# A gated linear attention with a feed-forward block on one core: eight small products over 128 rows instead of 32, and a new order table

## The chip, the cores and the metric

The kernel runs on one core of a Trainium2 chip. The metric is the time on the device in microseconds (us). Five engines work side by side, each through its own list in order: PE (matrix products, with the loads of its weights shown apart as PEld), DVE (vector work), ACT (activation functions, through tables that must be loaded), POOL (general work) and SP (here only the issuing of DMA transfers). PE writes to eight accumulation banks, called `banks`.

## What is computed

```python
mag = np.sqrt(a_re * a_re + a_im * a_im)
scale = np.minimum(mag, 0.999) / (mag + 1e-06)
...
for t in range(S):
    new_re = ar * S_re - ai * S_im
    new_im = ar * S_im + ai * S_re
    kv = np.einsum('bhd,bhe->bhde', k[:, :, t], v[:, :, t])
    S_re, S_im = (new_re + kv, new_im)
    y[:, :, t] = np.einsum('bhd,bhde->bhe', q[:, :, t], S_re)
...
xn = (x - mu) / np.sqrt(var + 1e-06) * g_ln
ch = np.maximum(xn @ w_ch1, 0.0) @ w_ch2
return (x + ch)
```

There are 4 batches of 8 heads, 768 steps and a head dimension of 48; x joins the heads to rows of 384, and the two weight matrices are 384 x 1536 and 1536 x 384. All inputs and the output are float32.

## The kernel before

**Tiling.** The 768 steps of a batch are cut into six chunks of 128. Two chunks (R = 2) make a pair P, three pairs make a batch, so there are 12 pairs and 24 chunks n. The recurrence is turned into products: with running sums of the logarithm of the decay and of the phase, a chunk's attention is a masked product of scaled queries and scaled keys, and a state G carries what earlier chunks left. Pair 0 is worked on in two halves of four heads (names such as `e.0.1`), all others whole (`e.3.0`).

**The steps of a pair,** by their names in the code and the lines where they are written:

- loads on SP: `are`, `aim` (L438), `k`, `q`, `vf` (L397)
- decays and phases: `ln`, `iv` (ACT, L441, L443), `r`, `r2`, `u`, `l`, `lc`, then on PE `dec` (L470), a running sum made by a product with the constant triangle u_e, whose exponentials are `e` and `en` (ACT, L474); `th` (ACT), `ph` (PE, L485 with pick and L489 with u_th), `car` (the phase carried to the next pair), `sin`, `cos`, with `qt` (PE, L514) or `abs` in between
- `ke`, `qe`, `ks`, `qs` multiply keys and queries by these; they run on DVE or POOL
- `dps` (PE, L565): eight small products, one per head, that turn the last row of `e` into a column; `decc` copies it to `dec`, which scales the state
- `kT`, `qT` (PE transposes, L584) and their copies `ksT`, `qsT`; `am` (L607), masked by `atm` on DVE; `gm` (L631) and the state `G`; `y` (L668, L671) and its copy `x`
- the feed-forward block: `bn`, `rstd`, `xtr` (PE, L689) with its copy `xT`, `mm1` in three groups of 512 columns (L722), `relu` into h (ACT L734 or DVE L736), `mm2` (L746), `ot` and, where POOL adds, `oa`, and the store `st` (L767).

A copy with the engine letter S in the table is a DMA transpose on SP's queue instead of a PE transpose and a copy (L589, L695); then the PE transpose isn't in the table.

**Once in the program.** Constants are made on POOL: u_e (`ue`), `pick`, `mask`, `ident`, zeros (`pad`, `zdec`), `car0`; `uth` on DVE is u_e over two pi. `wl.0` and `wl.1` are the two weight loads from POOL (L352, L354). `wp` (PE, L377) and `wc` (DVE, L381) fold the norm into the first weight matrix, which must be done before `mm1` can use it. `warm` are fillers: products on u_e of 512 columns (`warm.w`, L780) and of 256 (`warm`, L776) that nothing reads.

**The order.** PLAN is a table written out. Each entry is `step:engine bank`, and each engine runs its entries in the order of the table; waits between engines follow from the data. `@name` adds a wait: this step begins only when the step `name` is over. In the table before, the opening of PE's list reads

```
warm.w25:P2 warm.w26:P2 warm.w27:P2 warm.w28:P2 warm.3:P2@car.0.0 ... dec.0.0:P2
... wl.0:G@ke.0.0.0 ... mm1.0.1.0:P0 ... wl.1:G@mm1.0.1.0
```

Tiles come in rings (two or three buffers of most kinds), so a load of a later pair can be issued only when the step that read the buffer last is over.

Of the kernel before, what the change touches and what calls it, by code (L numbers as in the profile page):

```python
# [43 lines left out]
warm.w8:P0 warm.w9:P0 warm.w10:P0 warm.w11:P0 warm.w12:P0 warm.w13:P0 warm.w14:P0 warm.w15:P0 warm.w16:P0 warm.w17:P0
warm.w18:P0 warm.w19:P0 warm.w20:P0 warm.w21:P0 warm.w22:P0 warm.w23:P0 warm.w24:P0 warm.0:P0 warm.1:P0 warm.2:P0
ph.0.0:P1 aim.2.0:S r2.1.0:G@r2.0.0 ph.0.1:P0 q.0.1:S car.0.1:V0 car.0.0:V1 tab.log.2:A u.0.0:A u.0.1:A l.0.0:V
q.0.0:S u.1.0:A lc.0.0:V l.0.1:V warm.w25:P2 warm.w26:P2 warm.w27:P2 warm.w28:P2 warm.3:P2@car.0.0 warm.w29:P2
warm.w30:P2 warm.w31:P2 warm.4:P2 warm.5:P2 warm.6:P2 dec.0.0:P2 vf.0.1:S lc.0.1:V en.0.0:A2 l.1.0:V k.0.0:S ln.2.0:A
lc.1.0:V iv.2.0:A q.1.1:S warm.w32:P3 warm.w33:P3 warm.w34:P3 warm.w35:P3 warm.w36:P3 warm.w37:P3 warm.7:P3 warm.8:P3
dec.1.0:P4 pad.ks.1:G@lc.1.0 e.0.0:A2 r.2.0:V ph.1.0:P6 q.1.0:S en.1.0:A4 e.1.0:A4 dec.0.1:P2 r2.2.0:V k.1.1:S  # L50
qe.0.0.0:V e.0.1:A2 car.1.0:V6 are.3.0:S en.0.1:A2 warm.w38:P3 warm.w39:P3 warm.9:P3 warm.10:P3 warm.11:P3 dps.0:P4
v.0:V u.2.0:A qe.0.1.0:V aim.3.0:S decc.0:V4 ke.0.1.0:V q.2.0:S ke.0.0.0:V wl.0:G@ke.0.0.0 l.2.0:V tab.trig.3:A
sin.0.1:A0 q.2.1:S sin.0.0:A1 warm.w40:P3 warm.w41:P3 warm.w42:P3 warm.w43:P3 warm.12:P3@u.2.0 warm.w44:P3 warm.w45:P3
warm.w46:P3 warm.w47:P3 warm.w48:P3 warm.13:P3@ke.0.0.0 warm.14:P3 warm.15:P3 qt.0.1:P0 sin.1.0:A6 dps.1:P4 lc.2.0:V
qt.0.0:P1 ks.0.0.1:V dec.2.0:P2 qs.0.1.1:V cos.0.0:A1 qe.1.0.0:V cos.0.1:A0 qt.1.0:P6 qs.0.0.1:V th.2.0:A qs.0.0.0:V
qs.0.1.0:V ks.0.1.1:V cos.1.0:A6 warm.w49:P0 warm.16:P0 warm.17:P0 qT.1:P0 ks.0.0.0:V ks.0.1.0:V qT.0:P1 qsT.1:V0
decc.1:A4 ke.1.0.0:G@ks.0.1.0 kT.1:P5 qsT.0:V1 kT.0:P6 gm.0:P0 qe.1.0.1:V tab.log.4:A e.2.0:A2 qs.1.0.0:V ksT.1:V5
G.0:A0 ke.1.0.1:G@qs.1.0.0 en.2.0:A2 ksT.0:V6 warm.w50:P1 warm.w51:P1 warm.w52:P1 warm.w53:P1 warm.w54:P1 warm.18:P1
warm.19:P1 warm.20:P1 gm.1:P0 am.1:P4 ks.1.0.0:V ln.3.0:A ph.2.0:P2 ks.1.0.1:V iv.3.0:A atm.1:V4 qs.1.0.1:G@ks.1.0.1
kT.3:P6 kT.2:P7 G.1:V0 y.1:P4 ksT.2:V7 am.0:P0 wgc:G tab.trig.5:A sin.2.0:A2 qT.2:P5 k.2.0:S atm.0:V0 x.1:A4  # L60
warm.21:P7 qt.2.0:P2 xtr.1:P4 qsT.2:V5 cos.2.0:A2 wp.1:P7 vf.1.1:S r.3.0:G xT.1:V4 y.0:P0 ksT.3:A6 wc.1.2:V7 am.2:P2
vf.1.0:S qT.3:P1 wc.1.1:V7 x.0:A0 wp.0:P4 pad.qs.2:G k.2.1:S wc.1.0:V7 th.3.0:A xtr.0:P0 wp.2:P5 r2.3.0:G atm.2:V2
qsT.3:A1 are.4.0:S ph.3.0:P6 xT.0:A0 wc.2.1:V5 aim.4.0:S am.3:P2 qe.2.0.1:G car.3.0:A6 mm1.0.1.0:P0 wc.2.0:V5
sin.3.0:A6 are.5.0:S mm1.0.1.1:P0 atm.3:V2 wl.1:G@mm1.0.1.0 v.1:A qt.3.0:P6 vf.2.0:S relu.0.1:A0 ke.2.0.0:G wc.2.2:V5
gm.2:P2 y.2:P3 G.2:V2 cos.3.0:A6 ke.2.0.1:G mm1.0.2.0:P0 wc.0.2:V4 x.2:A3 y.3:P5 qe.2.0.0:G wc.0.0:V4 gm.3:P2 x.3:A5
mm1.0.2.1:P0 wc.0.1:V4 ks.2.0.1:G xtr.2:P3 xtr.3:P5 xT.2:A3 mm1.0.0.0:P6 xT.3:V5 relu.0.2:A0 bn.1:V mm1.1.0.1:P4
ks.2.0.0:V mm1.0.0.1:P6 bn.0:V qs.2.0.0:G@ks.2.0.0 mm1.1.2.0:P0 relu.0.0:V6 tab.log.6:A u.3.0:A kT.4:P3 mm1.1.0.0:P4
one:G ksT.4:V3 ln.4.0:A mm1.1.2.1:P0 qs.2.0.1:V relu.1.0:A4 gs.3:V2 mm1.1.1.1:P6 l.3.0:V iv.4.0:A kT.5:P2 qT.5:P5
relu.1.2:A0 lc.3.0:V mm1.1.1.0:P6 aim.5.0:S ksT.5:V2 G.3:G@lc.3.0 qT.4:P3 qsT.5:V5 relu.1.1:A6 dec.3.0:P0 qsT.4:V3
vf.2.1:S am.5:P4 e.3.0:A0 r.4.0:V am.4:P6 en.3.0:A0 dps.3:P3 atm.5:V4 mm2.1.0:P2 are.6.0:S r2.4.0:A mm2.1.1:P2  # L70
atm.4:V6 vf.3.0:S u.4.0:A mm2.1.2:P2 mm2.0.0:P0 rstd.0:A l.4.0:V ln.5.0:A k.3.0:S mm2.0.1:P0 lc.4.0:V iv.5.0:A
mm2.0.2:P0 decc.3:V3 k.3.1:S ot.1:V2 dec.4.0:P6 v.2:A r.5.0:G@lc.4.0 bn.3:V mm2.3.0:P5 e.4.0:A6 ot.0:V0 q.3.1:S
gm.4:P1 bn.2:V y.4:P3 en.4.0:A6 mm2.3.1:P5 q.3.0:S r2.5.0:G G.4:V1 ln.6.0:A mm2.3.2:P5 x.4:V3 vf.3.1:S iv.6.0:A y.5:P0
bn.4:V xtr.4:P1 mm2.2.0:P4 ke.3.0.0:G k.4.1:S x.5:V0 u.5.0:A xT.4:V1 mm2.2.1:P4 ke.3.0.1:G st.0:S xtr.5:P0 mm2.2.2:P4
xT.5:V0 rstd.1:G l.5.0:V k.4.0:S mm1.2.1.1:P0 tab.trig.7:A th.5.0:A mm1.2.1.0:P0 qe.3.0.1:V aim.6.0:S th.4.0:A
qe.3.0.0:V mm1.2.2.1:P2 relu.2.1:A0 qs.3.0.1:V q.4.0:S mm1.2.2.0:P2 ks.3.0.0:V q.4.1:S ph.4.0:P6 qs.3.0.0:V
relu.2.2:A2 ks.3.0.1:V are.7.0:S qT.6:P0 lc.5.0:V car.4.0:A6 bn.5:V kT.6:P1 ke.4.0.1:G@lc.5.0 abs.4.0:A6 ph.5.0:P2
ot.2:V4 q.5.1:S oa.3:A5 ke.4.0.0:G@lc.5.0 ksT.6:V1 sin.4.0:A6 kT.7:P4 qsT.6:V0 r.6.0:G vf.4.0:S qT.7:P1 cos.4.0:A
ksT.7:V4 mm1.2.0.0:P6 vf.4.1:S abs.5.0:A2 qsT.7:V1 mm1.2.0.1:P6 v.3:G sin.5.0:A2 dec.5.0:P0 relu.2.0:V6 st.2:S
cos.5.0:A qe.4.0.1:G am.7:P4 am.6:P2 th.6.0:A atm.7:V4 are.8.0:S ks.4.0.0:G gm.6:P6 mm2.4.0:P7 G.6:A6 mm2.4.1:P7  # L80
r2.6.0:A st.1:S atm.6:V2 mm2.4.2:P7 ot.3:G aim.7.0:S dps.4:P4 gm.7:P6 qe.4.0.0:G st.3:S decc.4:V4 y.7:P3 G.7:V6 y.6:P2
tab.log.8:A u.6.0:A mm2.5.0:P5 x.7:V3 rstd.2:G ks.4.0.1:V mm2.5.1:P5 x.6:A2 q.5.0:S en.5.0:A0 l.6.0:V xtr.6:P6 k.5.1:S
xtr.7:P2 kT.9:P4 v.4:A xT.6:V6 mm2.5.2:P5 xT.7:V2 lc.6.0:V e.5.0:A0 vf.5.1:S qs.4.0.1:V mm1.3.1.0:P2 ln.7.0:A ot.4:V7
qs.4.0.0:G@qs.4.0.1 dec.6.0:P0 ot.5:V5 mm1.3.1.1:P2 iv.7.0:A bn.7:V mm1.3.0.0:P6 ksT.9:A4 relu.3.1:V2 r.7.0:G qsT.8:S
qT.9:P5 en.6.0:A0 mm1.3.0.1:P6 qsT.9:V5 k.5.0:S e.6.0:A0 kT.8:P2 relu.3.0:V6 qe.5.0.1:G am.9:P4 st.4:S ln.8.0:A
mm1.3.2.1:P0 qe.5.0.0:G q.6.0:S atm.9:V4 r2.7.0:A mm1.3.2.0:P0 qs.5.0.0:G iv.8.0:A gm.8:P3 ph.6.0:P6 aim.8.0:S G.8:V3
u.7.0:A ksT.8:V2 y.9:P4 q.6.1:S relu.3.2:V0 qs.5.0.1:G mm2.7.0:P5 st.5:S gm.9:P3 mm2.7.1:P5 bn.6:V k.6.0:S
tab.trig.9:A th.7.0:A am.8:P0 ke.5.0.1:G mm2.6.0:P2 car.6.0:A6 atm.8:V0 rstd.3:G sin.6.0:A6 are.9.0:S mm2.7.2:P5
x.9:A4 mm2.6.1:P2 ke.5.0.0:V abs.6.0:A6 k.6.1:S gs.9:V3 y.8:P0 ks.5.0.0:V vf.5.0:S mm2.6.2:P2 x.8:A0 l.7.0:V dps.6:P1
qsT.10:S qT.11:P0 xtr.9:P3 lc.7.0:V xtr.8:P4 qsT.11:A0 ph.7.0:P6 ks.5.0.1:V ot.6:V2 q.7.1:S r.8.0:G@ks.5.0.1 xT.9:A3  # L90
kT.11:P0 ot.7:V5 xT.8:A4 kT.10:P2 st.6:S bn.8:V abs.7.0:A6 mm1.4.0.0:P4 ksT.10:V2 sin.7.0:A6 ke.6.0.0:G aim.9.0:S
mm1.4.0.1:P4 bn.9:V decc.6:A1 mm1.4.2.1:P2 th.8.0:A ke.6.0.1:G ksT.11:V0 mm1.4.2.0:P2 cos.6.0:A relu.4.0:V4 G.9:G
k.7.0:S mm1.4.1.0:P0 relu.4.2:A2 mm1.4.1.1:P0 ks.6.0.1:V vf.6.1:S v.5:V mm2.8.0:P4 relu.4.1:A0 car.7.0:V6 vf.7.1:S
ks.6.0.0:G@v.5 am.10:P2 am.11:P6 atm.10:V2 gm.10:P5 k.7.1:S mm2.8.1:P4 qe.6.0.1:G mm2.8.2:P4 G.10:V5 are.10.0:S
tab.log.10:A rstd.4:A ln.9.0:A atm.11:V6 qe.6.0.0:G kT.12:P2 st.7:S dec.7.0:P0 iv.9.0:A qs.6.0.0:V y.10:P3 vf.6.0:S
en.7.0:A0 qs.6.0.1:V y.11:P5 ph.8.0:P6 ksT.12:V2 r.9.0:G@qs.6.0.1 x.10:A3 qsT.13:S x.11:V5 e.7.0:A0 qT.12:P3 ot.8:V4
r2.8.0:A xtr.11:P2 xtr.10:P0 qsT.12:V3 mm2.9.0:P1 k.8.0:S ke.7.0.1:G u.8.0:A xT.11:V2 mm2.9.1:P1 xT.10:V0 st.8:S
# [719 lines left out]
```

## Time and profile before

| | us |
|---|---|
| median of three runs | 188.77 (188.55 to 188.9) |
| the profiled execution | 188.55 |
| its span, first to last instruction | 186.8 |
| ACT busy | 152.3 |
| POOL busy | 98.7 |
| fillers of 512 columns, 55 products, busy | 16.1 |
| `mm1` (L722), 432 products, busy | 51.5 |
| `mm2` (L746), 300 products, busy | 52.7 |
| `relu` on ACT, 24, mean of one | 1.02 |
| `relu` on DVE, 12, mean of one | 1.22 |

A row of the profile gives the line, the engine, what is written and what is read, the shapes, the count, the busy time, the mean time of one instruction in ns, and the idle time of the engine just before it with what ended that. Busy time counts overlapping instructions once; PE's products overlap, so the mean of one is longer than the distance between two. The granted clock is the share of full speed that PE was allowed; on this core it is 1.000 over the span.

### The profile page before, as it was taken

The numbers are of one execution on the slowest core, as the hardware profiler recorded it, in microseconds if no ns is written. First come the engines' busy times: TensorE is split into PE (matmuls) and PEld (weight loads), VectorE is DVE, ScalarE is ACT, GpSimd is POOL, SyncE is SP. The second block draws the span as 40 slices with busy tenths as digits, with TensorE's granted clock in tenths as the row PEclk, the third lists the DMA queues.
The fourth block names the chain that finished last, engine by engine and source line by source line (L and its number), as shares of the span: only waits on it lengthen the run. The fifth ranks groups of instructions, "written<-read, shape, count | busy, mean of one in ns | idle before, by whom it ended". The sixth has DMA issues, their size and how long they took to land.

```text
span 186.8 us, 5113 instructions
## 1 busy us (share of the span) xinstructions
PE 180.8 (97%) x2031; PEld 139.8 (75%) x2032; DVE 157.9 (84%) x287; ACT 152.3 (81%) x219; POOL 98.7 (53%) x117
## 2 busy tenths in 40 slices
...
PEclk9999999999999999999999999999999999999999
...
GB/s 157 281 234 214 254 192 216 235 249 199 219 148 171 255 177 194 166 146 228 231 147 231 230 227 207 173 252 222 206 218 139 149 177 228 173 139 170 39 112 86
DMA packets 124536, 35.93 MB, mean 192 GB/s; under 512 B 120544, under 2 KB 123744, under 8 KB 124512
## 3 DMA queue, kind: packets, MB, share of 16 engines
...
q8 instruction: 16, 0.26, 0.6%
...
## 4 chain that ended last, share of the span: by engine, by line
PE 76%; SPq 7%; DVE 7%; ACT 4%; issue 2%; DMA 2%; POOL 1%; POOLq 0%
PE banks L722 23%; PE banks L746 22%; SPq L397 6%; PE banks L584 5%; PE banks L780 5%; PE banks L607 5%; PE banks L489 3%; PE banks L470 2%; PE banks L668 2%; PE banks L631 2%; PE banks L671 2%; DVE w1b L381 2%; PE banks L689 2%; PE banks L485 2%; DMA k<-in_k_dram 2%
## 5 line engine op out<-in xcount | busy, mean ns | idle before, releaser
L746 PE MATMUL banks<-w2b,h 128*128 128x384 bf16 (+2 forms) x300 | 52.7, 319 | 0.0
L722 PE MATMUL banks<-xT,w1b 128*128 128x256 bf16 x432 | 51.5, 273 | 0.0
L722 PEld LDWEIGHTS <-w1b 128*128 128x128 bf16 x432 | 46.3, 114 | 1.1
L746 PEld LDWEIGHTS <-h 128*128 128x128 bf16 x300 | 27.0, 98 | 13.7 <-ACT h L734 0.2
L734 ACT ACTIVATE h<-banks 128x1024 bf16<-128x1024 f32 x24 | 24.4, 1023 | 10.9 <-PE banks L722 10.9
L288 DVE TENSOR_TENSOR atm<-banks,mask 128x1024 bf16<-128x1024 f32 x24 | 29.1, 1218 | 2.6 <-PE banks L607 2.4
L288 POOL TENSOR_TENSOR ke<-k,en 128x384 bf16<-128x384 f32 x19 | 17.2, 919 | 13.4 <-ACT h L734 5.1
L288 POOL TENSOR_TENSOR r<-aim,are 128x768 f16<-128x768 f32 x8 | 14.6, 1820 | 12.7 <-ACT are L443 9.7
L785 ACT ACT_TABLE_LOAD x15 | 19.2, 1283 | 1.0 <-PEq L801 0.8
L780 PE MATMUL banks<-u_e 128*128 128x512 f16 x55 | 16.1, 438 | 2.3 <-POOL u_e L316 2.2
L736 DVE TENSOR_SCALAR h<-banks 128x1024 bf16<-128x1024 f32 x12 | 14.6, 1216 | 4.0 <-PE banks L722 4.0
L288 POOL TENSOR_TENSOR qe<-q,e 128x384 bf16<-128x384 f32 x14 | 12.7, 917 | 7.6 <-DMA q<-in_q_dram 4.0
L759 POOL TENSOR_TENSOR ot<-ot,x 128x384 f32<-128x384 f32 x9 | 8.1, 914 | 16.0 <-ACT ot L751 11.4
L607 PE MATMUL banks<-qsT,ksT 128*128 128x128 bf16 x192 | 14.2, 219 | 0.0
L681 DVE BATCH_NORM_STATS2 stats<-x 128x6 f32<-128x384 bf16 x24 | 13.2, 551 | 0.3 <-ACT x L283 0.2
L607 PEld LDWEIGHTS <-ksT 128*128 128x128 bf16 x192 | 11.9, 98 | 1.7 <-DVE atm L288 0.2
L780 PEld LDWEIGHTS <-u_e 128*128 128x128 f16 x55 | 5.9, 109 | 9.1 <-issue 4.2
L459 DVE SCALAR_TENSOR_TENSOR l<-r,w 128x768 f16<-128x768 f16 (+1 forms) x13 | 12.1, 931 | 0.2 <-ACT r L455 0.2
L288 POOL TENSOR_TENSOR qs<-qe,trig 128x768 bf16<-128x768 bf16 x6 | 9.8, 1644 | 4.3 <-DVE qs L288 2.2
L441 ACT ACTIVATE w<-are 128x768 f32<-128x768 f32 (+1 forms) x13 | 10.2, 791 | 2.3 <-DMA are<-in_a_re_dram 2.3
L489 PE MATMUL banks<-th,u_th 128*128 128x384 f16 (+1 forms) x52 | 11.8, 313 | 0.0
L668 PE MATMUL banks<-v,atm 128*128 128x48 bf16 x192 | 11.8, 183 | 0.0
...
## 6 DMA issues: line engine op xcount, KB each, us to landing
...
```

Of the source, the lines that this page charges most:

```text
L288: {"DVE": nc.vector, "POOL": nc.gpsimd}[eng(name)].tensor_tensor(**kw)
L459: nc.vector.scalar_tensor_tensor(out=S_("l"), in0=S_("r2"), scalar=0.5, in1=S_("w"), op0=ALU.mult, op1=ALU.add)
L489: nc.tensor.matmul(heads(ps[:, c]), lhsT=u_th[:, c, j], rhs=step(T("th", P), j), start=False, stop=(j == R - 1), skip_group_check=True)
L607: nc.tensor.matmul(ps[:, h], lhsT=T("ksT", n)[:, h], rhs=T("qsT", n)[:, h], start=True, stop=True)
L668: nc.tensor.matmul(ps[:, h], lhsT=T("atm", n)[:, h], rhs=T("v", P)[:, c, h], start=True, stop=nfirst)
L681: nc.vector.bn_stats(out=T("stats", n), in_=T("x", n))
L722: nc.tensor.matmul(ps[:, jj], lhsT=w1b[:, dc, ts(gi, JG * C)].rearrange("k (p j) -> k j p", j=JG)[:, jj], rhs=T("xT", P)[:, dc].rearrange( ...
L734: act(out=dst, in_=src, func=AF.Relu)
L736: nc.vector.tensor_scalar(out=dst, in0=src, scalar1=0.0, scalar2=None, op0=ALU.max)
L746: nc.tensor.matmul(bank(f"o.{N}")[:, ws], lhsT=T("h", P)[:, j, ts(c, C)], rhs=w2b[:, j, ws], start=(j == 0), stop=(j == NJ - 1))
L780: g.add(f"warm.w{i}", lambda i=i: nc.tensor.matmul(bank(f"warm.w{i}"), lhsT=u_e[:, 0, 0], rhs=u_e.rearrange("p c j t -> p (c j t)"), start ...
L785: g.add(f"tab.{nm}.{i}", lambda tab=tab: nc.scalar.preload_act_table_set(tab))
```

## The change

The products of `dps` read all 128 rows of `e` and the whole last column of the identity, where they read the last 32 rows of both. Row 127 is the only one that the column doesn't meet with zero, before and after, so the result is the same.

```diff
-                                     lhsT=T("e", P)[96:C, R - 1, ts(h, D)],
-                                     rhs=ident[96:C, C - 1:C], start=True, stop=True)
+                                     lhsT=T("e", P)[:, R - 1, ts(h, D)],
+                                     rhs=ident[:, C - 1:C], start=True, stop=True)
```

Two more constants are made, u_ec on POOL and u_thc on DVE. They belong to another way of laying out `are` and `aim` (chunk by chunk, with a plain triangle) for the pairs in a set WHOLE. That set is empty, so the two loads, `dec` and `ph` are as before and the constants feed nothing.

```diff
+WHOLE = set()
...
+    u_thc = pool.tile([C, 2, C], FP16, name="u_thc")
+    u_ec = pool.tile([C, 2, C], FP16, name="u_ec")
...
+    def c_uec():
+        nc.gpsimd.memset(u_ec, 1.0)
+        nc.gpsimd.affine_select(out=u_ec[:, 0], in_=u_ec[:, 0], pattern=[[1, C]],
+                                compare_op=ALU.is_ge, fill=0.0, base=0, channel_multiplier=-1)
+
+    def c_uthc():
+        nc.vector.tensor_scalar(out=u_thc, in0=u_ec, scalar1=INV2PI, scalar2=None, op0=ALU.mult)
...
+            def sums(pairs, chunks, c):
+                if P in WHOLE:
+                    return [(chunks[:, 1 if j < c else 0], j, j == c) for j in range(c + 1)]
+                return [(pairs[:, c, j], j, j == R - 1) for j in range(R)]
...
-    for i in range(55):
+    for i in range(41):
```

PLAN is another table throughout: other orders on every engine, other banks, some steps on other engines. The fillers of 512 columns are 41 instead of 55; those of 256 stay 22; all 14 left out stood before the first `mm1`. `xtr.16` is gone and `xT.16` goes through SP. The counts that change by engine:

| step | before | after |
|---|---|---|
| `relu` | 24 ACT, 12 DVE | 28 ACT, 8 DVE |
| `ks` | 20 DVE, 6 POOL | 16 DVE, 10 POOL |
| `qe` | 10 DVE, 14 POOL | 7 DVE, 17 POOL |
| `ke` | 5 DVE, 19 POOL | 7 DVE, 17 POOL |
| `r` | 5 DVE, 8 POOL | 7 DVE, 6 POOL |
| `r2` | 4 DVE, 3 POOL, 6 ACT | 8 DVE, 1 POOL, 4 ACT |
| `v` | 3 DVE, 5 POOL, 4 ACT | 8 POOL, 4 ACT |
| `abs` | 8 ACT | 5 ACT, 3 DVE |
| `ot` | 16 DVE, 9 POOL (with `oa` on ACT) | 20 DVE, 5 POOL |
| `xT` | 16 DVE, 6 ACT, 2 SP | 14 DVE, 7 ACT, 3 SP |

The opening, cut to the entries that the prediction speaks of:

```diff
-warm.w25:P2 ... warm.3:P2@car.0.0 ... dec.0.0:P2 ... en.0.0:A2 ... ln.2.0:A ... iv.2.0:A
-wl.0:G@ke.0.0.0 l.2.0:V ... lc.2.0:V ... wp.1:P7 ... mm1.0.1.0:P0 ... wl.1:G@mm1.0.1.0
+warm.w26:P1 warm.3:P1 warm.4:P1 ph.1.0:P4 ... dec.0.0:P1 ... ln.2.0:A ... iv.2.0:A ... en.0.0:A1
+l.2.0:V ... lc.2.0:V wl.0:G@lc.2.0 ... wp.1:P5 ... mm1.0.1.0:P4 ... car.3.0:A2 mm1.0.1.1:P4 wl.1:G@car.3.0
```

More of the change, by code (lines that the diff above doesn't have):

```diff
@@ L44 @@
[L44 to L97, printed above, removed]
-bn.11:V ke.7.0.0:G mm2.9.2:P1 q.7.0:S bn.10:V am.12:P4 ks.7.0.1:G ot.9:V1 mm1.5.1.1:P2 tab.trig.11:A th.9.0:A
@@ L99 @@
-atm.12:V4 mm1.5.1.0:P2 abs.8.0:A6 q.8.1:S v.6:G mm1.5.2.0:P0 relu.5.1:V2 sin.8.0:A6 mm1.5.2.1:P0 q.8.0:S cos.7.0:A
-mm1.5.0.1:P4 l.8.0:V aim.10.0:S relu.5.2:A0 mm1.5.0.0:P4 are.11.0:S qe.7.0.1:V y.12:P6 cos.8.0:A lc.8.0:V gm.12:P2
-kT.13:P7 x.12:V6 qe.7.0.0:G@lc.8.0 vf.7.0:S dps.7:P3 relu.5.0:A4 ph.9.0:P0 ksT.13:V7 qs.7.0.1:G@lc.8.0 G.12:V2
-xtr.12:P4 decc.7:V3 am.13:P6 sin.9.0:A0 gm.13:P2 mm2.11.0:P5 atm.13:V6 rstd.5:G mm2.11.1:P5 ks.7.0.0:V mm2.11.2:P5
-tab.log.12:A ln.10.0:A G.13:V2 ksT.14:S y.13:P3 r2.9.0:V car.9.0:A0 mm2.10.0:P2 x.13:V3 iv.10.0:A mm2.10.1:P2
@@ L114 @@
-atm.16:V0 k.10.0:S mm1.7.1.1:P4 sin.10.0:A2 v.8:G vf.9.1:S mm1.7.0.1:P6 th.11.0:A car.10.0:V2 q.10.1:S mm1.7.2.1:P0
-G.15:V relu.7.1:A4 qs.9.0.1:V ph.11.0:P2 bn.14:V relu.7.0:A6 ke.10.0.1:G@qs.9.0.1 st.12:S gm.16:P4 mm1.7.2.0:P0
-ke.9.0.0:G@qs.9.0.1 cos.10.0:A G.16:V4 y.16:P7 vf.10.1:S relu.7.2:A0 am.17:P4 qe.10.0.0:V mm2.15.0:P6 atm.17:V4
-k.11.0:S sin.11.0:A2 mm2.15.1:P6 abs.11.0:A2 mm2.15.2:P6 ks.9.0.0:V qs.9.0.0:V cos.11.0:A dps.9:P3 y.17:P0 x.16:V7
-qsT.18:S mm2.14.0:P1 ks.9.0.1:V x.17:A0 decc.9:A3 xtr.16:P2 xtr.17:P0 qe.10.0.1:G@ks.9.0.1 mm2.14.1:P1 ksT.19:S
@@ new lines @@
+bn.2:V ksT.5:A7 qT.5:P1 l.3.0:V mm1.1.1.1:P2 are.5.0:S ksT.4:A6 qT.4:P0 lc.3.0:V relu.1.0:V4 mm1.1.1.0:P2 qsT.4:A0
+are.6.0:S r.4.0:G@lc.3.0 dec.3.0:P6 bn.3:V relu.1.1:A2 am.4:P4 aim.5.0:S bn.0:V mm2.2.0:P0 e.3.0:A6 q.3.0:S mm2.2.1:P0
+qsT.5:V1 v.2:G r2.4.0:A atm.4:V4 mm2.2.2:P0 G.3:G u.4.0:A am.5:P2 k.3.0:S mm2.0.0:P1 rstd.0:G atm.5:V2 rstd.1:A
+en.3.0:A6 gm.4:P4 mm2.0.1:P1 k.3.1:S ln.5.0:A l.4.0:V mm2.0.2:P1 y.4:P5 iv.5.0:A lc.4.0:V dps.3:P6 k.4.0:S G.4:V4
+dec.4.0:P2 ln.6.0:A x.4:V5 r.5.0:G@lc.4.0 y.5:P4 q.3.1:S en.4.0:A2 bn.4:V mm2.1.0:P5 ot.0:V1 x.5:A4 mm2.1.1:P5
@@ new lines @@
+decc.3:A6 qe.3.0.0:V e.4.0:A2 st.0:S mm2.1.2:P5 r2.5.0:V iv.6.0:A q.4.0:S xtr.4:P1 bn.5:V xtr.5:P4 ke.3.0.0:G@r2.5.0
+mm2.3.0:P6 u.5.0:A vf.3.1:S xT.4:V1 mm2.3.1:P6 xT.5:V4 ot.2:V0 mm2.3.2:P6 aim.6.0:S ke.3.0.1:V st.2:S mm1.2.1.1:P0
+ks.3.0.0:V tab.trig.7:A th.4.0:A dps.4:P2 qe.3.0.1:G@ks.3.0.0 mm1.2.1.0:P0 are.7.0:S decc.4:V2 th.5.0:A ot.1:V5
+ph.4.0:P2 l.5.0:V vf.3.0:S relu.2.1:A0 mm1.2.2.1:P4 ks.3.0.1:V sin.4.0:A2 mm1.2.2.0:P4 qs.3.0.1:V k.4.1:S qs.3.0.0:V
+car.4.0:A2 kT.6:P0 st.1:S relu.2.2:A4 ke.4.0.0:V qT.7:P1 abs.4.0:V2 kT.7:P7 r.6.0:G@ke.4.0.0 ksT.6:A0 ph.5.0:P4
@@ new lines @@
+k.5.0:S ksT.7:V7 cos.4.0:A qsT.7:V1 mm1.2.0.1:P2 q.4.1:S abs.5.0:A4 lc.5.0:V qT.6:P0 ot.3:V6 v.3:G@lc.5.0 q.5.0:S
+mm1.2.0.0:P2 sin.5.0:A4 qsT.6:V0 qe.4.0.0:G@lc.5.0 dec.5.0:P6 are.8.0:S th.6.0:A relu.2.0:V2 am.7:P0 k.5.1:S
+ke.4.0.1:G cos.5.0:A am.6:P4 atm.7:V0 mm2.5.0:P2 q.5.1:S mm2.5.1:P2 r2.6.0:V aim.7.0:S mm2.5.2:P2 atm.6:V4 tab.log.8:A
+e.5.0:A6 qe.4.0.1:G@r2.6.0 mm2.4.0:P3 u.6.0:A rstd.2:G ks.4.0.1:V gm.6:P0 vf.4.0:S mm2.4.1:P3 G.6:A0 ks.4.0.0:V y.6:P1
+qs.4.0.0:V k.6.1:S mm2.4.2:P3 x.6:A1 l.6.0:V en.5.0:A6 y.7:P4 gm.7:P0 xtr.6:P1 lc.6.0:V x.7:A4 kT.8:P5 qs.4.0.1:V
@@ new lines @@
+qs.5.0.1:G dps.6:P2 gm.8:P7 ph.6.0:P4 G.8:V7 tab.trig.9:A th.7.0:A atm.8:V0 y.9:P3 qe.6.0.0:G qsT.10:S sin.6.0:A4
+mm2.6.1:P6 decc.6:V2 mm2.6.2:P6 l.7.0:V x.9:A3 car.6.0:A4 are.9.0:S y.8:P1 abs.6.0:A4 qT.11:P0 ks.5.0.1:G@l.7.0
+vf.5.1:S x.8:V1 ph.7.0:P2 qsT.11:V0 st.5:S xtr.9:P0 xtr.8:P5 ke.6.0.1:G car.7.0:A2 kT.11:P1 xT.9:V0 xT.8:A5 k.7.0:S
+ot.6:V6 gm.9:P7 abs.7.0:A2 kT.10:P0 r.8.0:G bn.9:V mm1.4.2.1:P4 sin.7.0:A2 bn.8:V aim.9.0:S mm1.4.2.0:P4 cos.7.0:A
+gs.9:V7 mm1.4.0.1:P2 ke.6.0.0:G ksT.11:V1 q.6.1:S cos.6.0:A mm1.4.0.0:P2 ksT.10:V0 v.5:G r2.8.0:A mm1.4.1.1:P6
```

139 lines of the change are left out of this document (95 added, 44 removed).

## The prediction

> **What bounds the kernel now.** I read the page's busy shares first, then the busy time of each engine in stretches, then the groups by shape, then the order of time around one of the products that change.
>
> ```profile
> PE 180.8 (97%) x2031; PEld 139.8 (75%) x2032; DVE 157.9 (84%) x287; ACT 152.3 (81%) x219; POOL 98.7 (53%) x117
> ...
> PEclk9999999999999999999999999999999999999999
> ```
>
> ```profile
> 12.00:25.00 13.00, 12.38 (x92) 6.52 (x90) 11.77 (x28) 12.16 (x21) 1.53 (x2) 1.00 1.06 230
> 25.00:38.00 13.00, 12.88 (x170) 9.33 (x169) 12.80 (x21) 11.97 (x19) 8.79 (x8) 1.00 1.07 226
> 38.00:60.00 22.00, 21.90 (x276) 17.93 (x274) 21.45 (x41) 20.79 (x30) 11.43 (x11) 1.00 0.95 195
> 60.00:90.00 30.00, 30.00 (x358) 24.06 (x357) 27.78 (x50) 29.19 (x40) 21.94 (x23) 1.00 0.84 194
> ```
>
> The columns are the stretch, its length, then PE, PEld, DVE, ACT, POOL busy, the granted clock, the DMA share and GB/s. From 38 us on PE is never idle, and the chain of waits is PE from 126.95 us to 184.00 us almost without a break. So the order of work after 45 us costs what PE's products cost. Before 38 us DVE and ACT are as full as PE, and part of PE's work there is filler: products on u_e whose result nobody reads.
>
> ```profile
> L780 PE MATMUL banks<-u_e 128*128 128x512 f16 x55 | 16.1, 438 | 2.3 <-POOL u_e L316 2.2
> L631 PE MATMUL banks<-v,ks 128*128 128x48 bf16 x160 | 7.3, 183 | 0.1
> L776 PE MATMUL banks<-u_e 128*128 128x256 f16 x22 | 4.1, 274 | 0.5 <-DVE ke L288 0.5
> L565 PE MATMUL banks<-ident,e 32*48 32x1 bf16 x64 | 2.8, 161 | 0.0
> ```
>
> A product's mean overlaps its neighbours, so I price a product by the distance from its start to the next one's: 216 ns for 512 columns at full clock, 162 for 384, 109 for 256, 56 for 128, 25 for 48 or 1. By these prices all products of the program take 173.2 us; the rest of the time up to 184 us is 2.2 us before the first product and 8.3 us of waits and surcharges, of which 2.7 us are the first 13 fillers at half pace, and only 2.0 us lie after 45 us. Most of these 2.0 us is one thing:
>
> ```profile
> 72.21 1.30 PE L746 MATMUL banks<-w2b,h 128*128 128x384 bf16 x7
> 73.44 0.35 PE L565 MATMUL banks<-ident,e 32*48 32x1 bf16 x8
> 73.73 0.37 PE L631 MATMUL banks<-v,ks 128*128 128x48 bf16 x8
> ```
>
> ```profile
> 73.03 0.10 PEld L746 LDWEIGHTS <-h 128*128 128x128 bf16 x1
> 73.44 0.27 PEld L565 LDWEIGHTS <-e 32*48 32x48 bf16 x8 [0.32 <-issue]
> 73.73 0.26 PEld L631 LDWEIGHTS <-ks 128*128 128x128 bf16 x8
> ```
>
> The last L746 product starts at 73.19 us, so the next could start at 73.35. The first of the eight L565 products starts at 73.44 (92 ns late), the second 45 ns behind it instead of 25, and what follows them starts 66 ns late. Nothing is awaited: the weight load, otherwise ahead of its product by many, stood still for 0.32 us. That is 178 ns of surcharge for each dps step.
>
> **The change part by part.**
>
> 1. *dps over 128 rows.* 8 steps of 8 products keep their count and their single column. If the surcharge goes, a step costs 8 x 25 = 0.20 us, as L631's eight do, instead of 0.38. Six of the eight steps lie after 45 us: 6 x 0.178 = **-1.07 us**. The two in the opening lie where PE also waits for others and count nothing. The trace has no product with 128 rows and fewer than 128 weight columns, so the bounds are -1.07 and 0. Evidence by rows: L485's products over 96 rows cost 0 to 4 ns extra on entry, L514's over 1 row and all 128 columns cost 96 and 90. Few rows suffice for a surcharge, few columns are not shown to. I take -1.07. Adding 96 rows that meet zeros of ident adds no time: L631 with 128 rows also runs at 25 ns.
>
> 2. *xtr.16 goes, xT.16 becomes a DMA transpose.* Three transposes of 56 ns: **-0.17 us**; DVE loses a copy of 0.35. On SP's queue it costs an issue of 1.2 us (the two xT transposes there now) and lands 2.3 us later; it stands behind st.11 and st.12, before qsT.19. PE has mm2.15, xtr.17 and mm2.14 in between, some 4 us. Without that cover mm1.8 would wait up to 3.5 us.
>
> 3. *u_ec and u_thc* feed nothing, since WHOLE is empty. POOL: a memset (0.21 to 0.53 by its neighbours) and a select of 0.41 at most; DVE 0.29 at most. DVE stands idle to 7.20 us for aim, POOL from 7.48 to 9.92. pick moves behind them: POOL's list reaches its end at 0.79 + 7.5 = 8.3 us, and the first ph needs it at 10.6. Cost 0; without the cover about 1 us on the first ph.
>
> 4. *14 fillers fewer before the first mm1*, 14 x 216 = 3.0 us of PE. Whether that time comes off is decided by what the first mm1 waits for. The real products before mm1.0.1.0 are the same set in both orders. On DVE wc.1.0, the last scaling it needs, moves behind 2.1 us more work: atm.2 (1.22), ke.1.0.0 and ke.1.0.1 (0.55 each), ksT.3 (0.68), r2.1.0 and uthc come in; v.0, qe.1.0.0 and xT.1 go out. r2.1.0 and uthc (0.6) fall into DVE's wait of 2.09 us for the first phases; the wait of 0.78 at 16.38 for iv.2.0 goes, as ACT now does iv.2.0 ahead of en.0.0. DVE needs 36.35 + 1.5 - 0.8 = 37.1 us where it needed 36.35. On ACT a ksT copy (1.0) leaves for DVE, an xT copy (0.5) comes, and the wait of 0.41 for en.0.0 goes: xT.0, ready at 37.39 now, could be ready at 36.5, but x.1 has to follow y.1, which PE's list ends at 33.0: x.1 to 33.4, cos.2.0 to 34.25, xT.1 (behind xtr.1) to 34.9, x.0 to 35.3, th.3.0 to 36.15, qsT.3 to 37.1, xT.0 to 37.5. So the first mm1 starts near 37.7 instead of 37.99, and y.2, gm.3 and y.3 behind it hang on atm.3 and G.2, which DVE ends 0.2 us later than now. I count **0**; bounds: -3.0 if the fillers were all that PE did there, +0.7 if the old DVE waits stay. The removed fillers turn into idle time in pieces of 0.4 to 1.2 us. The nearest row is the 0.48 us before 21.51 us, across which the granted clock stays 1.00.
>
> 5. *wl.0 turns behind lc.2.0* instead of ke.0.0.0. POOL issues it at 21.77 now and it lands 9.6 us later, before wp.1 at 33.34. lc.2.0 ends 0.5 to 1.3 us later than ke.0.0.0 did by DVE's list, so the weights land at 31.9 to 32.6. wp.1 still comes behind y.0, at about 33.5. Cost 0, cover 0.9 us. Behind wl.0 on POOL stand pad.qs.1 and qe.1.0.0, which have a turn of their own behind ks.1.0.0, near 25.6, so nobody waits for them earlier. wl.1 turns behind car.3.0 at about 38.7, now 39.12; mm2 starts at 51.4 instead of 52.2, against a landing at 50.5.
>
> 6. *Everything after 45 us in another order.* The other remaining waits there are 2.0 - 1.07 = 0.9 us (the largest 0.23 at 126.6 and 0.20 at 130.6). By the durations of the rows DVE's list is 154.3 us long instead of 158.2 (relus, an r2 and copies change engines both ways), ACT's 155.0 instead of 154.2, POOL's 101.0 instead of 100.6. Up to the first mm1 of pair 3, where it is tightest, DVE now has 38.3 us of work beside 38.4 us of PE, afterwards 39.3 beside 40.0. I take the waits as unchanged, **0**; bounds -0.9 and +3 (below).
>
> Sum: -1.07 - 0.17 = -1.24. The profiled execution took 188.55 us, 186.8 of it in the span; it gives 187.31. The median shown is 0.22 above that execution, so **187.5 us**.
>
> **The rivals.**
>
> *The surcharge stays,* because the products still use 48 weight columns. For: entering L565 from L514 costs 88 ns and the way back 65, though both have few rows, so more than the row count may be in it. Against: L514 alone pays at full columns. Then -0.17 is left: 188.6, no change. [...]
>
> *The relus lose their cover: slower.* PE's list gives the time between a group's last mm1 and the first mm2 that reads its relu. In pairs 1 to 9 four relus have less than 1.8 us now (1.75, 1.75, 1.75, 1.70); afterwards eight have (relu.1.1, 3.2, 6.0 near 1.75, 9.2 1.70, and 2.0, 4.1, 5.0, 8.0 at 1.55 to 1.58). A relu takes 1.02 us on ACT and 1.22 on DVE. So it is decided at 0.3 to 0.5 us: where ACT or DVE still has an operation of 0.8 (e, sin, ln) in hand, PE stops. If half of the eight come one such operation late, 4 x 0.8 - 4 x 0.3 = 2.0 us, and PE has nothing to catch up with; with a few shorter waits for copies, 0.4 more: 189.9. For: DVE and ACT are over 90% busy from 38 to 90 us. Against: today's order with four such places waits 0.9 us in all.
>
> *The fillers come off.* If the opening is bound by PE's list, 3.0 us more go: 184.5; half of it 186.0. For: PE is 95% busy from 12 to 25. Against: DVE is 97% busy from 25 to 38, with more ahead of the first mm1 than now.
>
> **How the numbers follow.** The forecast 0.40, surcharge stays 0.17, relus 0.33, fillers 0.10. A measurement of this kernel tells 0.2% from no change, here 188.39 to 189.15. Faster: 0.38 of the forecast, 0.05 of the second case, all 0.10 of the last, 0.53. Same: 0.02 + 0.09 + 0.02 = 0.13. Slower: 0.03 + 0.31 = 0.34. The forecast's own range is 186.6 to 188.4 (0.9 us of waits either way); to leave out no more than 2 in 10 it is stretched to 185.8 on the side of the fillers and to 190.3 on that of the relus.
>
> **What would show it.** Step 1: the eight L565 products 25 ns apart, the next line's start 0.20 us after the first of them, no idle weight load ahead. Step 4: the first L722 product between 37.3 and 38.3 us; earlier by over 1 us is the fillers' case. Step 5: no idle PE just ahead of the first L377 or L746 product. Step 6: PE's waits after 45 us at about 0.9 us; waits of L746 on h would be the relus' case. The prediction is wrong if PE's list after 45 us is not what sets the end, or if waits there grow past 1.2 us.

## The result and the profile after

The changed kernel took 188.25 us (median; 187.60 to 188.99), the kernel before 188.70 on the same chip: a ratio of 0.9957 (0.9941 to 0.9973), 0.4% faster. The ratio goes by all runs, whose means are 188.13 and 188.94 us; the medians alone lie 0.24% apart. The profiled execution took 187.81 us with a span of 186.0, against 188.55 and 186.8. The last PE product ends at 182.51 us instead of 183.96.

In the changed kernel L494 is `dec`, L498 `e` and `en`, L589 `dps`, L655 `gm`, L746 `mm1`, L770 `mm2`, and L800 and L804 are the fillers of 256 and 512 columns. The page of the changed kernel, its busy shares and its row of the granted clock:

```profile
PE 177.2 (95%) x2015; PEld 138.7 (75%) x2015; DVE 155.5 (84%) x284; ACT 153.3 (82%) x219; POOL 100.9 (54%) x118
...
PEclk9999999999999999999999999999999999999998
```

The 8 at the end of the clock's row is the time from 184.57 us on, after PE's last product; it alone makes the mean clock of this execution 0.996.

The changed kernel by stretches (length, PE, PEld, DVE, ACT, POOL busy, granted clock, DMA share, GB/s):

```profile
12.00:25.00 13.00, 10.61 (x77) 5.75 (x76) 12.44 (x30) 12.67 (x23) 1.00 (x1) 1.00 1.06 211
25.00:38.00 13.00, 12.33 (x173) 9.35 (x171) 12.84 (x20) 11.09 (x16) 8.81 (x9) 1.00 1.02 211
38.00:60.00 22.00, 22.00 (x279) 18.32 (x277) 21.35 (x42) 20.95 (x31) 13.12 (x13) 1.00 0.86 186
60.00:90.00 30.00, 30.00 (x355) 24.19 (x354) 27.92 (x50) 29.03 (x40) 18.57 (x18) 1.00 0.94 214
```

From 38 us on PE is full, as before. Between 12 and 25 us it was busy for 12.38 us and is now for 10.61: the fillers left out became idle time. Where it stands is seen in the order of time (from 15.5 us on), and in the groups by shape:

```profile
15.25 0.81 PE L494 MATMUL banks<-l,u_e 128*128 128x384 f16 x4
17.48 0.34 PE L589 MATMUL banks<-ident,e 128*48 128x1 bf16 x8 [1.41 <-ACT en L498]
18.18 1.02 PE L804 MATMUL banks<-u_e 128*128 128x512 f16 x4 [0.36 <-ACT en L498]
```

```profile
L804 PE MATMUL banks<-u_e 128*128 128x512 f16 x41 | 12.4, 448 | 2.6 <-POOL u_e L319 2.2 <-ACT en L498 0.4
L655 PE MATMUL banks<-v,ks 128*128 128x48 bf16 x160 | 7.2, 183 | 0.0
L800 PE MATMUL banks<-u_e 128*128 128x256 f16 x22 | 4.1, 274 | 0.2
L589 PE MATMUL banks<-ident,e 128*48 128x1 bf16 x64 | 2.9, 165 | 1.4 <-ACT en L498 1.4
```

PE waits 1.41 us for the exponentials ahead of the first step of it and 0.36 us behind it, with no filler in either place. The products of `dps` read 128 rows, in 2.9 us against 2.8 before: no gain. The products around the step at 61.86 us (PE above, the weight loads below) show the same picture as before:

```profile
61.11 0.82 PE L746 MATMUL banks<-xT,w1b 128*128 128x256 bf16 x6
61.86 0.36 PE L589 MATMUL banks<-ident,e 128*48 128x1 bf16 x8
62.15 0.85 PE L746 MATMUL banks<-xT,w1b 128*128 128x256 bf16 x6
```

```profile
60.95 0.71 PEld L746 LDWEIGHTS <-w1b 128*128 128x128 bf16 x6
61.85 0.28 PEld L589 LDWEIGHTS <-e 128*48 128x48 bf16 x8 [0.19 <-issue]
62.15 0.58 PEld L746 LDWEIGHTS <-w1b 128*128 128x128 bf16 x6
```

Six L746 products at 109 ns end their turn at 61.77 us; the first L589 product starts at 61.86, the next 45 ns behind it, and L746 comes back at 62.15, 0.29 us after the first of eight products that need 0.20. The weight load again stands still, for 0.19 us, and waits for nothing.

So the gain came from elsewhere. Distances between starts, less the price of each product (216, 162.5, 109, 56 and 25.3 ns for 512, 384, 256, 128 and fewer columns), give it, before against after:

- The first `mm1` starts at 37.63 us instead of 37.99: -0.37.
- From there to 45 us waits and surcharges shrink from 0.57 to 0.22 us: -0.35.
- Three transposes fewer: -0.17.
- After 45 us waits and surcharges together fall from 2.01 to 1.45 us: -0.57. The six steps of `dps` keep theirs, 1.22 and 1.19 us; all other waits went from 0.79 to 0.26. The largest of before, 0.16 to 0.23 us at 118.3, 126.6 and 130.6 us, are gone; the largest that is left is 0.07 us at 65.5 us.

These make -1.46; the last product's end moved by -1.45. Behind it 0.63 us were lost: from there to the end of the span before took 2.88 us, now 3.51. Which of the moves in the table shortened the waits no run separates.

The 22 runs of the changed kernel fall into two groups. Ten had a mean granted clock of 0.996 or more, with a median of 187.77 us; twelve had 0.987 to 0.991, with a median of 188.39. A median below is therefore to be read with the number of its runs at full clock.

### The profile page after: what moved, and what is told of

Same layout as the page of the kernel before. It is cut to its first block, busy times and chain, and to the rows that moved or that the text cites. A ratio compares the mean times of both kernels' runs of the same rounds, so it can differ in the third digit from the quotient of the medians.

```text
span 186.0 us, 5078 instructions
## 1 busy us (share of the span) xinstructions
PE 177.2 (95%) x2015; PEld 138.7 (75%) x2015; DVE 155.5 (84%) x284; ACT 153.3 (82%) x219; POOL 100.9 (54%) x118
## 4 chain that ended last, share of the span: by engine, by line
PE 83%; DVE 7%; ACT 4%; DMA 2%; issue 2%; DVEq 0%
PE banks L746 26%; PE banks L770 25%; PE banks L608 7%; PE banks L631 6%; PE banks L494 3%; PE banks L513 3%; PE banks L692 3%; PE banks L655 2%; PE banks L695 2%; PE banks L713 2%; DMA are<-in_a_re_dram 2%; PE banks L509 2%; DVE l L483 1%; PE banks L589 1%; PE banks L390 1%
## 5 line engine op out<-in xcount | busy, mean ns | idle before, releaser
L746 PE MATMUL banks<-xT,w1b 128*128 128x256 bf16 x432 | 52.5, 273 | 0.0
L770 PE MATMUL banks<-w2b,h 128*128 128x384 bf16 (+2 forms) x300 | 52.2, 319 | 0.0
L746 PEld LDWEIGHTS <-w1b 128*128 128x128 bf16 x432 | 45.9, 114 | 1.0 <-DVE xT L286 0.2
L770 PEld LDWEIGHTS <-h 128*128 128x128 bf16 x300 | 27.0, 97 | 14.6 <-DVE h L760 0.2
L758 ACT ACTIVATE h<-banks 128x1024 bf16<-128x1024 f32 x28 | 28.3, 1023 | 10.3 <-PE banks L746 10.2
L289 POOL TENSOR_TENSOR ks<-ke,trig 128x768 bf16<-128x768 bf16 x10 | 16.4, 1643 | 7.2 <-DVE l L486 3.3
L289 POOL TENSOR_TENSOR ke<-k,en 128x384 bf16<-128x384 f32 x17 | 15.5, 918 | 7.5 <-ACT x L284 2.4
L289 POOL TENSOR_TENSOR qe<-q,e 128x384 bf16<-128x384 f32 x17 | 15.5, 917 | 4.7 <-DVE ks L289 1.9
L289 POOL TENSOR_TENSOR r<-aim,are 128x768 f16<-128x768 f32 x6 | 11.0, 1836 | 10.1 <-DVE ke L289 3.5
L785 DVE SCALAR_TENSOR_TENSOR ot<-banks,rstd,x 128x384 f32<-128x384 f32 (+2 forms) x20 | 11.7, 591 | 5.1 <-PE banks L770 2.6
L804 PE MATMUL banks<-u_e 128*128 128x512 f16 x41 | 12.4, 448 | 2.6 <-POOL u_e L319 2.2
L284 ACT CAST x<-banks 128x384 bf16<-128x384 f32 x15 | 7.2, 480 | 7.5 <-PE banks L695 7.0
L692 PEld LDWEIGHTS <-atm 128*128 128x128 bf16 x192 | 10.9, 96 | 1.9 <-issue 0.3
## 6 DMA issues: line engine op xcount, KB each, us to landing
w2b<-in_moe_w_ch_dram POOLq DMA_DIRECT2D x1, 1152.0 KB, 11.4
```

Of the source, the lines that this page charges most:

```text
L289: {"DVE": nc.vector, "POOL": nc.gpsimd}[eng(name)].tensor_tensor(**kw)
L692: nc.tensor.matmul(ps[:, h], lhsT=T("atm", n)[:, h], rhs=T("v", P)[:, c, h], start=True, stop=nfirst)
L746: nc.tensor.matmul(ps[:, jj], lhsT=w1b[:, dc, ts(gi, JG * C)].rearrange("k (p j) -> k j p", j=JG)[:, jj], rhs=T("xT", P)[:, dc].rearrange( ...
L758: act(out=dst, in_=src, func=AF.Relu)
L770: nc.tensor.matmul(bank(f"o.{N}")[:, ws], lhsT=T("h", P)[:, j, ts(c, C)], rhs=w2b[:, j, ws], start=(j == 0), stop=(j == NJ - 1))
L785: nc.vector.scalar_tensor_tensor(out=o, in0=bank(f"o.{N}")[:, ws], scalar=T("rstd", P)[:, ds(c, 1)], in1=xs, op0=ALU.mult, op1=ALU.add)
```

## The experiments

**Rows alone undone.** The changed kernel with the 32 rows of before: what is left is the order table.

```diff
-lhsT=T("e", P)[:, R - 1, ts(h, D)],  rhs=ident[:, C - 1:C]
+lhsT=T("e", P)[96:C, R - 1, ts(h, D)],  rhs=ident[96:C, C - 1:C]
```

> The changed kernel with dps over the last 32 rows again, all else kept: the order table alone. Theory (the surcharge follows the 48 weight columns as well as the few rows, so the change of rows gave nothing): the eight products still stand 92 ns late on entry, 45 ns between the first two and 66 ns late on exit, the last product of PE ends at 182.5 us as in the changed kernel, and the time is 188.25 within 0.3. Rival (the 128 rows saved a part of it, and the order less than it seems): 0.3 to 1.1 us slower, 188.6 to 189.3.

Measured: 188.17 us (187.57 to 188.74), a ratio of 0.9965 (0.9948 to 0.9982), as for the whole change; seven of its eleven runs had the low clock, twelve of 22 there. With the first product behind it a step pays 183 to 206 ns over eight times 25 ns after 45 us, against 187 to 213 in the changed kernel, and the last product ends at 182.40 us. The 96 more rows gave nothing; the whole gain is the order's.

**128 weight columns.** The tile `e` gets 80 more columns (zeros), and each `dps` product loads 128 columns from its head's first on. The further rows of its result are not read.

```diff
-"e": ([C, R, DM], BF16)
+"e": ([C, R, DM + 128 - D], BF16)
...
-nc.tensor.matmul(bank(f"dps.{P}")[0:D, ds(h, 1)], lhsT=T("e", P)[:, R - 1, ts(h, D)],
+nc.tensor.matmul(bank(f"dps.{P}")[0:128, ds(h, 1)], lhsT=T("e", P)[:, R - 1, ds(h * D, 128)],
```

> The changed kernel with dps over 128 weight columns: each product loads 128 columns of e from its head's first one on (the tile gets 80 columns of zeros behind the last head), and the copy reads the first 48 rows of the result as before. Theory (few columns alone bring the surcharge): the 178 ns of each step go, six of them after 45 us, 1.07 us; PE's last product ends at 181.4 us and the time is 187.2. Rival (the surcharge belongs to products with one moving column, or to the change of the bank): it stays, 188.25. Second rival (wider weight loads cost more): slower than 188.25.

Measured: 186.89 us (186.69 to 188.07), ratio 0.9907 (0.9889 to 0.9926). The order of time on PE in its profile (the lines are one further down, L590 is `dps`, L771 `mm2`; the last row is cut at 63 us):

```profile
51.65 2.11 PE L771 MATMUL banks<-w2b,h 128*128 128x384 bf16 x12 [1.02 <-DMA w2b<-in_moe_w_ch_dram]
...
62.13 0.82 PE L747 MATMUL banks<-xT,w1b 128*128 128x256 bf16 x6
62.79 0.34 PE L590 MATMUL banks<-ident,e 128*128 128x1 bf16 x8
62.99 0.28 PE L747 MATMUL banks<-xT,w1b 128*128 128x256 bf16 x1
```

Here the step starts 0.66 us behind the six L747 products' start, their own time, and L747 comes back 0.20 us later: eight times 25 ns and nothing else. The surcharge goes with the 48 columns, not with the 32 rows. The median flatters the edit, since five of the six runs had the full clock: the four of these without a long wait took 186.69 to 186.92 us, where the runs of the changed kernel at full clock have a median of 187.77, 0.9 us more. The profiled execution, 188.07 us, was the longest of the six: the second weight matrix was issued at 39.01 us as in the changed kernel but took 12.6 us to land instead of 11.4, and PE stood 1.02 us before the first `mm2`. In the changed kernel it landed at 50.44, and the first `mm2` started at 50.48: a cover (the time between a landing and its use) of 0.04 us.

**xT.16 back on PE and DVE.** One DMA less on SP; it was to show whether that DMA made the 0.63 us at the end.

```diff
-xT.16:S
+xtr.16:P3 ... xT.16:V3
```

> The changed kernel with the transpose of x.16 back on PE and its copy on DVE, one DMA less on SP. In the changed kernel the program ended 1.55 us after its last store had landed, in the one before 0.9 us after it: SP waits for the DMA semaphores two at a time, in a fixed order, and the last store fell on a semaphore of the second of six waits instead of the last. Theory (which semaphore the last store gets is decided by the count of the transfers issued before it): with one transfer less it falls on the last wait again, 0.6 us go, 0.17 us of PE come: 187.8. Rival (the end is not tied to the count): 188.25 + 0.17 = 188.4.

Measured: 187.68 us (187.46 to 188.35), ratio 0.9954 (0.9935 to 0.9972). Five of its six runs had the full clock, with a median of 187.61 us beside the 187.77 of the changed kernel's: no clear difference. SP ends the program with six waits, each for two semaphores, in a fixed order. The last store was signalled on the sixth of them before, on the second in the changed kernel, and on the sixth again here, so the theory was right on that. But from that store's landing to the end the three profiles show 0.92, 1.54 and 1.35 us: 0.2 us came back, not 0.6. In the changed kernel 0.61 us pass from the landing to the end of the sixth wait, 0.35 of them as a gap ahead of that wait. Before, the same gap of 0.35 us lies ahead of the landing and costs nothing, and 0.05 us are left. Here it lies ahead of the landing too, but another gap of 0.36 us stands behind the sixth wait. What makes these gaps stays open.

**No fillers in the opening.** The 34 fillers behind the first two `ph` steps are out of the table (of the 63 that the change has).

```diff
-warm.w26:P1 warm.3:P1 warm.4:P1 ... warm.w30:P6 ... warm.20:P0 warm.21:P0
```

> The changed kernel without the 34 fillers behind the first two ph steps (15 of 512 columns, 19 of 256, 5.3 us of PE). Theory (the opening is set by DVE and ACT, the fillers only lie in PE's waits): the first mm1 stays at 37.6 us and the time at 188.25 within 0.4, as long as the granted clock stays at 1; if the idle stretch of 3.5 us between dps.1 and qt.0.1 takes the clock down to a half, what PE does from 21 us on takes twice as long for a while and the first mm1 comes 1 to 3 us later: 189.3 to 191. Rival (fillers are in PE's way): 1 to 3 us faster, 185.3 to 187.3.

Measured: 188.89 us (188.47 to 189.65), ratio 1.0016 (1.0002 to 1.003). The mean granted clock was 0.973 to 0.982 in all twelve runs. The clock row of its page, and two stretches of it:

```profile
PEclk9998559999999999999999999999999999999999
```

```profile
10.00:17.70 7.70, 4.86 (x44) 3.48 (x43) 6.33 (x15) 7.40 (x13) 0.67 (x2) 1.00 1.14 223
17.80:27.90 10.10, 6.71 (x45) 4.72 (x45) 8.37 (x21) 8.80 (x15) 4.02 (x6) 0.50 1.11 223
```

From 17.73 to 27.97 us the clock is 0.50. The first `mm1` starts at 39.12 us, 1.5 later than in the changed kernel, though 34 products fewer stand ahead of it: the second case of the theory, at a smaller cost in time than the 189.3 to 191 us expected. Where the fillers stood PE now waits for ACT and DVE, 3.3 us in the longest place: they were not in its way, and they held the clock. In the 3.41 us up to 17.73 us, a third as long as the 10.24 us at half pace, PE was at work for 1.48 us, from 14.79 to 15.93 with a running sum and from 17.35 with `dps`.

**Small fillers into the new gaps.** 28 fillers of 128 columns, 22 ahead of `dps.1` and 6 behind it.

```diff
+    for i in range(28):
+        g.add(f"warm.s{i}", lambda i=i: nc.tensor.matmul(
+            bank("dec.0.1")[:, 384:512], lhsT=u_e[:, 0, 0], rhs=u_e[:, 1, 0],
+            start=True, stop=True), needs=["ue"], ps=("dec.0.1", 1))
...
-dps.1:P1
+warm.s0:P3 ... warm.s21:P3 dps.1:P1 warm.s22:P3 ... warm.s27:P3
```

> The changed kernel with 28 more fillers of 128 columns (56 ns each), 22 ahead of dps.1 and 6 behind it, where PE stood idle for 1.4 and 0.4 us; they write columns of the bank of dec.0.1 that nothing else uses. Of the 22 timed runs of the changed kernel 9 lie at 187.6 to 187.9 with a granted clock of 0.996 to 1.0, and 13 at 188.15 to 189.0, 12 of them with 0.987 to 0.991, which is one window of 3.4 us at half pace. Theory (the thinned fillers leave an opening so idle that the clock falls for one window in some runs): with the idle filled the clock stays, all runs lie near 187.7, and so does the median. Rival (the slow runs are those in which the second weight matrix lands late): two groups as before, median 188.2. Second rival (fillers there delay the chain): over 188.3.

Measured: 187.90 us (187.67 to 188.20), ratio 0.9948 (0.9928 to 0.9968). The granted clock was 0.997 to 1.000 in all eight runs, where 12 of 22 were below 0.992 without them. Of the other kernels without them it was seven of eleven runs with the 32 rows, seven of twelve in the next experiment, and one of six each with 128 columns and with xT.16 on PE: 28 of 57 in all. With the fillers it is none of the 20 timed runs of this kernel and of the two further down that have them. So the idle time before and behind `dps.1` is what cost the clock. The best runs got no better: they are the runs that had the full clock already.

**The second weight matrix earlier.**

```diff
-wl.1:G@car.3.0
+wl.1:G@th.3.0
```

> The changed kernel with the load of the second weight matrix behind th.3.0 instead of car.3.0, some 3 us earlier. In the profile of the changed kernel it landed at 50.44 us and the first mm2 started at 50.48; in that of e2 it landed at 51.61 and PE waited 1.17 us for it. Theory (late landings hit single runs only, the clock makes the slow group): the profile shows the landing 2 to 3 us ahead of the first mm2, the runs still fall into two groups, median 188.2 within 0.3. Rival (the landing makes the slow group): all runs near 187.7.

Measured: 188.41 us (187.67 to 189.83), ratio 0.998 (0.9957 to 1.0003): unclear against before, and no gain over the changed kernel. The load is issued at 36.36 us instead of 39.01 and so lands at 47.4. The runs are again in two groups: five at full clock, four of these at 187.67 to 187.90, and seven at 0.987 to 0.991, 188.19 to 189.83. One at full clock took 188.96 us; it has no trace, and what held it is open.

**All three together:** 128 columns, the small fillers, the earlier load.

```diff
-lhsT=T("e", P)[:, R - 1, ts(h, D)],
+lhsT=T("e", P)[:, R - 1, ds(h * D, 128)],
...
-dps.1:P1
+warm.s0:P3 ... warm.s21:P3 dps.1:P1 warm.s22:P3 ... warm.s27:P3
...
-wl.1:G@car.3.0
+wl.1:G@th.3.0
```

> The changed kernel with all three: dps over 128 weight columns, the fillers of e5, the earlier load of e6. Theory: six surcharges less, 1.07 us, on the undisturbed 187.7, and neither the half window nor a late landing: 186.6, all runs within 0.3 of it. Rival (the parts share a gain, or the earlier load disturbs loads that are needed sooner): 187.0 to 187.7.

Measured: 186.97 us, ratio 0.9897 (0.987 to 0.9925); five of six runs within 186.92 to 187.00. The sixth, 190.62 us at full clock, is not in the ratio; it has no trace, and what held it is open.

**The same with 64 and with 96 columns,** one execution each; the edit for 64 is shown, that for 96 has the other number, and the width of `e` and the rows of the result go with it.

```diff
-ds(h * D, 128)
+ds(h * D, 64)
```

> The kernel of e7 with 64 weight columns in dps instead of 128. [...] Rival (the surcharge belongs to 48 columns, which are no multiple of 32): no surcharge.

> 96 weight columns, the 28 extra fillers and the earlier load of w2b; with 64 columns the surcharge of 93 ns before and some 85 ns behind each step of dps was there, with 128 it was not. [...] Rival (anything below the full 128 columns pays): 88 to 94 ns before the first product of each step after 45 us, 1.0 us in all, 187.9 to 188.1.

Measured: 188.38 us with 64 columns, 187.58 with 96, both at full clock. PE in the order of time with 64 columns (the last row is cut at 63 us), and below it with 96 (L593 is `dps` and L750 `mm1` in both):

```profile
61.49 0.82 PE L750 MATMUL banks<-xT,w1b 128*128 128x256 bf16 x6
62.24 0.41 PE L593 MATMUL banks<-ident,e 128*64 128x1 bf16 x8
62.58 0.63 PE L750 MATMUL banks<-xT,w1b 128*128 128x256 bf16 x4
```

```profile
61.13 0.82 PE L750 MATMUL banks<-xT,w1b 128*128 128x256 bf16 x6
61.78 0.48 PE L593 MATMUL banks<-ident,e 128*96 128x1 bf16 x8
62.13 0.82 PE L750 MATMUL banks<-xT,w1b 128*128 128x256 bf16 x6
```

With 64 columns the step starts 0.75 us behind the start of the six, so 93 ns late, and its own products are 32 ns apart: 242 to 267 ns over the bare 200. With 96 it starts on time and the way back is free, but the products are 45 ns apart: 142 to 160 ns over. With 128 columns they are 25 ns apart; five of the six steps after 45 us pay 3 to 48 ns, the sixth 60 to 67. Neither rival came as written: with 64 columns the 93 ns on entry were there, with 96 they were not, and 187.58 us lies below the 187.9 to 188.1 foretold. The stop on entry and exit ends between 64 and 96 columns: 93 ns on entry at 48 and 64 columns, 0 at 96 and 128 in the steps shown. Of 96 and 128 only the 128 have the short distance between products, 25 ns for 45. What in PE makes the stop and the distances, the runs do not show; they give the times alone.

**128 columns and the small fillers, the load left where it was.** The edit against the kernel with all three:

```diff
-wl.1:G@th.3.0
+wl.1:G@car.3.0
```

> 128 weight columns and the 28 extra fillers, with the load of w2b left where the changed kernel has it. Theory (the surcharge of 178 ns goes with the 128 columns, the fillers keep the granted clock at 0.997 or more, and the earlier load of w2b in the version with all three edits was worth nothing): runs at 186.7 to 187.0 with the clock at 0.997 or more in all of them, ratio 0.990. Where a run has w2b landing later than 50.5, PE waits at the first mm2 and the run is up to 1.2 us longer. Rival (the earlier load is needed, since without the surcharge mm2 starts 0.4 us sooner): a wait for w2b in most runs, 187.4 to 188.1.

Measured: 186.86 us (186.72 to 187.00), ratio 0.9896 (0.9874 to 0.9919), clock 0.996 to 1.000 in all six. This beats both kernels. Beside the version with the small fillers alone, 187.90 us and also at full clock throughout, it differs in the columns only: 1.04 us, where six surcharges of 178 ns make 1.07. Its opening, with the gap ahead of `dps.1` filled:

```profile
15.24 0.81 PE L498 MATMUL banks<-l,u_e 128*128 128x384 f16 x4
16.38 1.39 PE L808 MATMUL banks<-u_e 128*128 128x128 f16 x22 [0.33 <-ACT e L502]
17.61 0.34 PE L593 MATMUL banks<-ident,e 128*128 128x1 bf16 x8
17.81 0.49 PE L808 MATMUL banks<-u_e 128*128 128x128 f16 x6
18.16 1.02 PE L812 MATMUL banks<-u_e 128*128 128x512 f16 x4
```

In its trace the second weight matrix landed in 10.4 us and nobody waited for it. The earlier load was worth nothing in these runs; the wait of 1.02 us was seen once in the five profiles of kernels that issue it at 38.9 to 39.1 us in the new order. From the first `mm1` to the end of the last product this version takes 144.03 us, the changed kernel 144.88, the kernel before 145.97.

## Why the prediction held, and where it was wrong

The time lay 0.75 us above the 187.5 us foretold, inside the forecast's own range and on the side foretold, but not by the step that was to bring it. That the number came so close is luck: the -1.07 of step 1 stayed away, and the new order gave 1.29 us in places that the sum had set to 0. The terms of the sum beside what was measured in the profiled executions:

| term | predicted, us | measured, us |
|---|---|---|
| 1, `dps` over 128 rows | -1.07 | 0.0 |
| 2, xtr.16 | -0.17 | -0.17 |
| 3, two unused constants | 0 | 0 |
| 4, first `mm1` | 0 (start near 37.7) | -0.37 (37.63) |
| 6, waits after 45 us | 0 | -0.57 |
| from the first `mm1` to 45 us | none | -0.35 |
| behind the last product | none | +0.63 |
| outside the span | none | +0.09 |
| the execution | 187.31 | 187.81 |

**Step 1 failed** at "Few rows suffice for a surcharge, few columns are not shown to. I take -1.07." That no line of the profile had the case was taken for its costing nothing. L514 differs from its neighbours in rows only and pays (96 and 90 ns); L565 differed in both. That showed that few rows suffice, and left the columns untested, and they suffice too: with 128 rows and 48 columns 93 ns on entry remain, with 128 columns none. The rival of 0.17, "The surcharge stays", had the cause, the 48 columns; its time of 188.6 missed because it added the -0.17 alone and no gain by the order.

**Step 6** had the sign of its term unresolved, "bounds -0.9 and +3", and took 0. The measured -0.57 lies well towards the lower end. The working for the relus' rival counted eight places with little cover, and none of them waited: no wait of `mm2` on h stands in the trace after 45 us. Cover of 1.55 to 1.75 us against a relu of 1.0 to 1.2 was enough here.

**Step 4** was right on the start, 37.63 for 37.7, but not by the two steps that it named as the last. xT.0 was ready at 37.36 us and wc.1.0 at 36.37 (foretold 37.5 and 37.1), and PE came to the first `mm1` in its own order, without a wait since 31.68 us. Up to there the chain that ended last runs mostly over DVE, so the fillers' case (earlier by over 1 us) did not come. It should have booked the 0.3 us that its own number gave. It was wrong on the clock. "The removed fillers turn into idle time in pieces of 0.4 to 1.2 us. The nearest row is the 0.48 us before 21.51 us, across which the granted clock stays 1.00": the largest piece is 1.41 us with 0.36 close behind, and in 12 of 22 runs the clock fell, to a mean of 0.987 to 0.991. Between the two groups lie 0.6 us. The median stands 0.44 above the profiled execution for that reason, and not 0.22 as was assumed from before.

**Step 5** was right in that nobody waited in the changed kernel: the first load, issued at 21.24 us, landed at 31.89 (foretold 31.9 to 32.6). The second landed at 50.44, foretold 50.5. But `mm2` started at 50.48 and not at 51.4, as all of PE ran ahead, so the cover was 0.04 us and not 0.9.

**Not foreseen** was the end: 0.63 us behind the last product. There the last store falls on an early one of SP's closing waits; putting it back on the last gave 0.2 us, as a gap came up elsewhere, and the rest is open. Without this loss the profiled execution would have come out below the sum, at some 187.2 us for 187.31.
